# Decoding of weight pieces fenced behind the recurrence's copies, loads six and decodes three ahead

## The chip, the cores and the metric

The kernel runs on one core of a Trainium2 chip. The metric is the device time of one execution in microseconds; the median of three runs is compared.

## The reference

Two parts follow each other. The first is a recurrence over 768 steps for each of 4 batches and 8 heads, with a state of 40x40:

```
for t in range(S):
    y[:, :, t] = einsum('bhd,bhde->bhe', r_t, state)
    Sa = einsum('bhde,bhe->bhd', state, a_t)
    state = state * w_t[:, :, None, :] - einsum('bhd,bhe->bhde', Sa, b_t)
    state = state + einsum('bhd,bhe->bhde', v_t, k_t)
```

Its result, as 3072 tokens of 320 numbers, goes through two dense blocks with float64 weights: `h = ((x @ w1) * (x @ w2)) @ w3 @ w_out` (inner size 1024), and then `relu(h @ w_in) ** 2 @ w_out2` (inner size 2048).

## The kernel before, in words

The 768 steps are cut into 24 chunks of 32 steps, which are computed in closed form. A **preparation** of a chunk p reads its image (im, iw; L541, L551), scans the decay on VectorE (`prep_scan`: suf L556, gc L562, inv L564, wi L566), multiplies on GpSimd (`prep_mul`: L578, L584 four times), stores AW_d (L585, L586), and takes two products on TensorE (`prep_pq` L597 with the copies Pn on ScalarE L601, qt on VectorE L602 and GpSimd L604 and the store Q_d L605; `prep_kb` L614 with the copy kn on ScalarE L618 and the store KB_d L619). A **solve** (L645 to L668, VectorE) inverts the triangular matrices of four chunks at once (tmp L656, T L659, transposed into tt at L662); a **corner** (TensorE L690 and L693, ScalarE x L697 and tt L701) completes one chunk's inverse in the first four chunks.

The chain of a chunk c is: `do_x0` (TensorE L742, ScalarE copy X0 at L744), `do_sa` (L752, ScalarE copy SA at L754), `do_sat` (transposition L759, ScalarE copies vs L761 and YI L764 four times), `do_l` (L772, VectorE YI L777), `do_z` (L785, ScalarE YR L788; not in chunk 0), and `do_ys` (L800, VectorE RX L808, which is the state for the next chunk, and yst L812, stored to X_d at L815). `load_x`, `load_rv` and `load_y` fetch the next chunk's inputs.

Between the stages TensorE does other work, taken from a queue (`Fill`) by the nanoseconds of the tables GAP0 to GAPE: first the **fold** of w3 and w_out into one matrix (L462, sixteen pieces of w3 with four steps each), then the tiles of 256 tokens of the first dense block (`a_tile`: loads xf, xr L381 and L383; splits L357 to L360; products ab L370 with copies and products L401 and L402, gh and gl L407 and L408; px L428). TensorE's order is the program's order; on the other engines a scheduler places the instructions by priority and by its own times, and each engine then works in order. All loads and stores that appear below are issued in order by SP on one queue.

The weights come as 64-bit numbers and are **decoded** on the chip (`fetch`): a load by SP (L319), one ScalarE instruction for the high words (L325), one for the low words in place (L326), and two VectorE instructions that join them (L328, L330). A piece of w1, w2 or w_in is then split in two parts by ScalarE (L340, L353) and GpSimd (L341, L354). The tile that holds a raw piece is called raw or, where it borrows a place that is used later for something else, early; wst is the decoded piece. Before the change `fetch` does load and decoding in one call: five pieces of w3 ahead of the recurrence (W3_FIRST), one more per piece used, and the ten pieces of w1 and w2 in two batches, at the eighth and the thirteenth step of the fold (SPLIT_AT). The **change-over** to the second dense block (the loop that calls `split_w`, `split_r` and `wu` after the last chunk in the program) decodes w_in and w_out2; its first pieces find free buffers and are placed from chunk 3 on.

`FIRST` and `SECOND` are priorities of the stages and preparations; decoding has none:

```
            if kind == "decode":
                fn()
            else:
                with self.tc.high_priority(offset=FIRST):
                    fn()
```

`tc.issue_after(x)` keeps an instruction behind x in the order; before the change it is used for VectorE's decoding behind the first solve (`hold`).

## Time and profile before

| | |
|---|---|
| runs | 1069.87, 1073.65, 1074.45 us; median 1073.65 |
| profiled execution | 1071.28 us, span 1069.5 us, mean clock of TensorE 0.961 |
| busy | TensorE 918.1 us (86%), VectorE 712.5 (67%), ScalarE 443.8 (41%), GpSimd 233.2 (22%) |
| start of chunk (L742) | 0: 59.0; 1: 97.8; 2: 128.4; 3: 174.1; 4: 205.1; 5: 236.7; 12: 403.8; 13: 427.2; 23: 652.0 us |

A line of the timeline gives the start and the length of an instruction (or of a run of like ones) in microseconds, the engine, the line of the kernel, the operation, the tiles written and read, and in brackets how long the engine had been idle and what ended it. The engines are PE (TensorE), DVE (VectorE), ACT (ScalarE), POOL (GpSimd) and SP. An arrow with DMA means that a load or store ended the wait. The chunks are of unequal length in the beginning, 38.8 us for the first and 23 to 28 for those from the fifth on.

### The profile page before, as it was taken

How to read it: one execution, taken by the hardware profiler on the slowest of the kernel's cores; microseconds unless marked ns; L12 is line 12 of the kernel's file. 1: busy time of each engine (PE TensorE's matmuls, PEld its weight loads, DVE VectorE, ACT ScalarE, POOL GpSimd, SP SyncE). 2: the span in 40 equal slices, each digit the busy share in tenths (PEclk: the TensorE clock that was granted, in tenths of full speed). 3: DMA queues.
4: the chain of work that ended last, by engine and by line, in shares of the span. 5: the costliest groups of instructions: out<-in, count | busy, mean ns of one | idle time of the engine just before them, and what ended most of it. 6: DMA issues, size and time to landing. Idle time of an engine off the chain costs nothing.

```text
span 1069.5 us, 29225 instructions
## 1 busy us (share of the span) xinstructions
PE 918.1 (86%) x12240; PEld 822.5 (77%) x12240; DVE 712.5 (67%) x1399; ACT 443.8 (41%) x942; POOL 233.2 (22%) x304
## 2 busy tenths in 40 slices
PE   1327777688989889979899999889999999999997
PEld 1315545588888878979798889868989898898896
DVE  6864879957975997798489444887456554444432
ACT  2424556343434423424343434775334333333332
POOL 0271224433343343533200000652000000000000
PEclk9999888899999999989899999989999999999999
DMA  8976785666666567766644542665122121000001
GB/s 212 307 235 177 209 247 158 171 168 170 163 154 173 148 151 182 170 170 149 164 118 110 136 96 60 171 188 111 30 62 53 59 48 25 2 25 1 18 8 28
DMA packets 208922, 134.45 MB, mean 126 GB/s; under 512 B 143741, under 2 KB 184062, under 8 KB 208368
## 3 DMA queue, kind: packets, MB, share of 16 engines
q1 hardware_dynamic: 201424, 110.61, 40.6%
q0 software_dynamic: 7072, 21.57, 7.1%
q8 instruction: 99, 1.62, 0.7%
q10 hardware_dynamic: 288, 0.33, 0.2%
q14 instruction: 39, 0.32, 0.1%
HBM read 99.27 MB, written 33.19 MB: 124 GB/s over the span
## 4 chain that ended last, share of the span: by engine, by line
PE 48%; DVE 26%; DMA 12%; issue 5%; ACT 4%; POOL 3%; SPq 2%; ACTq 0%; DVEq 0%; POOLq 0%
PE ph L370 16%; PE po L997 15%; PE ab L370 6%; DMA im<-img 5%; DVE tmp L656 4%; PE px L428 4%; DVE T L659 4%; PE pat L800 2%; DVE RX L808 2%; DVE yst L812 2%; DVE gl L408 2%; DVE g L402 1%; DVE wst L328 1%; DVE YI L777 1%; POOL im L584 1%
## 5 line engine op out<-in xcount | busy, mean ns | idle before, releaser
L997 PE MATMUL po<-wul,rh 128*128 128x320 f32 x384 | 118.3, 308 | 0.0
L997 PE MATMUL po<-wuh,rh 128*128 128x320 f32 x384 | 118.0, 308 | 0.0
L997 PE MATMUL po<-wuh,rl 128*128 128x320 f32 x384 | 116.9, 308 | 0.0
L407 ACT CAST gh<-g 128x256 fp32r<-128x256 f32 x96 | 39.0, 406 | 99.8 <-DVE g L402 86.5
L370 PE MATMUL ph<-xh,wih 128*128 128x512 f32 x192 | 76.0, 396 | 0.7 <-issue 0.7
L428 PE MATMUL px<-wph,gh 128*128 128x320 f32 x192 | 68.1, 355 | 9.3 <-DVE x L433 4.8
L370 PE MATMUL ph<-xh,wil 128*128 128x512 f32 x192 | 75.7, 394 | 0.0
L370 PE MATMUL ph<-xl,wih 128*128 128x512 f32 x192 | 75.6, 394 | 0.0
L997 PEld LDWEIGHTS po<-wul,rh 128*128 128x128 f32 x384 | 72.0, 188 | 4.2
L997 PEld LDWEIGHTS po<-wuh,rh 128*128 128x128 f32 x384 | 72.0, 188 | 3.8
L997 PEld LDWEIGHTS po<-wuh,rl 128*128 128x128 f32 x384 | 71.6, 188 | 0.6 <-DVE rl L984 0.6
L800 PE MATMUL pat<-YI,YR 128*40 128x72 f32 (+1 forms) x1536 | 58.8, 240 | 13.7 <-DVE qt L602 8.1
L800 PEld LDWEIGHTS pat<-YI,YR 128*40 128x40 f32 x1536 | 54.5, 127 | 19.2 <-DVE qt L602 9.7
L408 DVE TENSOR_TENSOR gl<-g,gh 128x256 fp32r<-128x256 f32 x96 | 48.2, 503 | 30.0 <-ACT gh L407 29.6
L401 ACT COPY a_sb<-ab 128x256 f32<-128x256 f32 x96 | 35.6, 371 | 76.4 <-PE ab L370 75.9
L656 DVE TENSOR_TENSOR tmp<-PT,T 128x31 f32<-128x31 f32 (+20 forms) x170 | 64.9, 382 | 3.4
L659 DVE TENSOR_TENSOR T<-T,tmp 128x31 f32<-128x31 f32 (+20 forms) x170 | 64.5, 380 | 3.0
L428 PE MATMUL px<-wph,gl 128*128 128x320 f32 x192 | 63.2, 329 | 3.4 <-DVE gl L408 3.4
L584 POOL TENSOR_TENSOR im<-im,suf 104x256 f32<-104x256 f32 x80 | 64.4, 836 | 0.0
L428 PE MATMUL px<-wpl,gh 128*128 128x320 f32 x192 | 62.4, 325 | 0.0
L370 PE MATMUL ph<-xq,wir 128*128 128x512 f32 x192 | 60.1, 394 | 0.0
L370 PE MATMUL ab<-xh,w1h 128*128 128x256 f32 x192 | 57.9, 302 | 2.5 <-ACT xh L357 2.2
(539 smaller groups left out, 2444.3 us busy)
## 6 DMA issues: line engine op xcount, KB each, us to landing
...
```

What stands on the lines that cost most here:

```text
L370: mm(out=ps, lhsT=seq[i][0], rhs=seq[i][1], start=(i == 0), stop=(i == 7))
L401: act.copy(out=a_sb, in_=ps[:, 0])
L407: act.copy(out=t["gh"][:, ff], in_=g)
L408: dve.tensor_tensor(out=t["gl"][:, ff], in0=g, in1=t["gh"][:, ff], op=ALU.subtract)
L428: mm(out=ps, lhsT=a_, rhs=b_, start=(k == 0 and i == 0), stop=(k == 7 and i == 2))
L584: eng.tensor_tensor(out=kb[:, g, :, :, j], in0=kb[:, g, :, :, j], in1=sg, op=ALU.mult)
L656: dve.tensor_tensor(out=tv, in0=Pv[:, :, s, s + 1:n].unsqueeze(3).to_broadcast(sh), in1=Tv[:, :, s, 0:s + 1].unsqueeze(2).to_broadcast(sh) ...
L659: return dve.tensor_tensor(out=o, in0=o, in1=tv, op=ALU.subtract).ins
L800: mm(out=ps[64 * y:64 * y + D, b, 72 * z:72 * z + n], lhsT=YR[:, u], rhs=YI[:, u, 0:n], start=True, stop=True, tile_position=(0, 64 * y))
L808: dve.tensor_tensor(out=o, in0=v[r, :, :, C:72], in1=decay.unsqueeze(3).to_broadcast([D, 2, HZ, D]), op=ALU.mult)
L812: dve.tensor_tensor(out=yst[r, :, 2 * g:2 * g + 2].rearrange("p z b t -> p b z t"), in0=v[r, :, :, 0:C], in1=wt[c][r, 2 * g:2 * g + 2, :, ...
L997: mm(out=po[j][g], lhsT=a_, rhs=b_, start=(ff == 0 and i == 0), stop=(ff == 15 and i == 2))
```

## The change

It has five parts.

- In the table BETWEEN the products of preparation 5 (`("pq", 5)`) go from behind `do_x0` of chunk 0 to behind `do_ys` of chunk 0.
- `fetch` only loads; a new `decode` does the four instructions. w3 is loaded six pieces ahead and decoded three ahead (AHEAD). The ten pieces of w1 and w2 are loaded one per w3 piece from the fourth on (SPLIT_FROM), each decoded two pieces later.
- A fence: the copies X0, SA and YI put themselves into `fence`, and ScalarE's two instructions of a decode are issued after the last of these in program order (`behind(fence)`).
- The first a_tile's load and split count as decoding, and the split is fenced also; they stand in the queue ahead of the fold's last two columns ("last").
- For the change-over the fence is the last YI copy of chunk 12 (MID), so that ScalarE's decoding of w_in and w_out2 stands behind it.

```diff
@@ BETWEEN
-    (0, "x0"): (("corner", 0), ("pq", 5)),
+    (0, "x0"): (("corner", 0),),
@@
-    (0, "ys"): (("kb", 5), ("pq", 6), ("kb", 6)),
+    (0, "ys"): (("pq", 5), ("kb", 5), ("pq", 6), ("kb", 6)),
@@
-SPLIT_AT = (8, 13)
-W3_FIRST = 5
-FOLD_STAGED = 8
-SPLIT_STAGED = 8
+AHEAD = 3
+SPLIT_FROM = 3
@@ fetch, decode
-            hold = []
+            hold, fence = [], []
+            behind = lambda x: tc.issue_after(x[-1]) if x else nullcontext()
...
-                act.activation(out=o, in_=hi.bitcast(F32), func=AF.Copy, scale=2.0 ** -112)
-                act.activation(out=lo, in_=lo, func=AF.Copy, scale=2.0 ** -29, bias=LOW)
-                with tc.issue_after(hold[-1]) if hold else nullcontext():
+                with behind(fence):
+                    act.activation(out=o, in_=hi.bitcast(F32), func=AF.Copy, scale=2.0 ** -112)
+                    act.activation(out=lo, in_=lo, func=AF.Copy, scale=2.0 ** -29, bias=LOW)
+                with behind(hold):
                     dve.scalar_tensor_tensor(out=ou, in0=ou, scalar=3, in1=lo, op0=ALU.logical_shift_left,
                                              op1=ALU.bitwise_or)
@@ a_tile
                 def split():
+                  with behind(fence if n == 0 else ()):
...
-                fill.push((0, load, "load"), (0, split, "load"), before="x")
+                fill.push((0, load, "load" if n else "decode"), (0, split, "load" if n else "decode"),
+                          before="x" if n else "last")
@@ fold
+                for i in range(3):
+                    load_w3(i)
...
+                for i in range(AHEAD):
+                    decode_w3(i)
+                    load_w3(i + 3)
...
+                for i in range(16):
+                    f = i // 2
+                    for k in range(4 * (i % 2), 4 * (i % 2) + 4):
+                        items.append((FOLD_NS, lambda f=f, k=k: step(f, k), "last" if f > 5 else "w"))
+                    if i + AHEAD < 16:
+                        then(decode_w3, i + AHEAD)
+                    if i + AHEAD + 3 < 16:
+                        then(load_w3, i + AHEAD + 3)
+                    m = i - SPLIT_FROM
+                    if 0 <= m - 2 < 10:
+                        then(decode12, m - 2)
+                    if 0 <= m < 10:
+                        then(load12, m)
@@ do_x0, do_sa, do_sat
-                    act.activation(out=X0, in_=ps[:, 0, 0:320].rearrange("p (h d) -> p h d", d=D),
-                                   func=AF.Copy, scale=-1.0)
+                    fence[:] = [act.activation(out=X0, in_=ps[:, 0, 0:320].rearrange("p (h d) -> p h d", d=D),
+                                               func=AF.Copy, scale=-1.0).ins]
...
+                        fence[:] = [act.copy(out=YI[96:128, H * b:H * b + H, C:72],
+                                             in_=SA[32 * b:32 * b + 32, :, 0:D]).ins]
+                    if c == MID:
+                        mid.extend(fence)
@@ change-over
+            fence[:] = mid
...
-                for k in range(2):
-                    split_w(wst, win, wih, wil, j, k)
+                todo = [piece_w(win, wih, wil, 256, j, k) for k in range(2)]
...
+                for load, split in todo:
+                    split(decode(wst, load(wst)))
```

What this does to the order of the engines shows at three places.

ScalarE, chunk 0, from the copies of preparation 4 to SA; before (L326 are low words of w_out and w3, early and raw their tiles):

```order
L601 COPY Pn<-pat 128x2x4x32
L326 ACTIVATE early<-early 128x512
L618 COPY kn<-pat 128x8x40 x2
L326 ACTIVATE early<-early 128x512
L744 ACTIVATE X_101<-pat 128x320
L697 ACTIVATE x_683<-pat 128x128
L701 COPY tt<-pat 16x8x16 x4
L325 ACTIVATE wst<-raw 128x512
L326 ACTIVATE raw<-raw 128x512 x3
L601 COPY Pn<-pat 128x2x4x32
L326 ACTIVATE raw<-raw 128x512
L754 COPY SA<-pat 128x8x40
```

And with the change, where the numbers of the lines are some 16 higher (L760 is X0, L770 SA, L781 YI, L778 vs):

```order
L617 COPY Pn<-pat 128x2x4x32
L634 COPY kn<-pat 128x8x40 x2
L760 ACTIVATE X_101<-pat 128x320
L713 ACTIVATE x_675<-pat 128x128
L717 COPY tt<-pat 16x8x16 x4
L770 COPY SA<-pat 128x8x40
L781 COPY YI<-SA 32x8x40 x4
L778 COPY vs<-pat 104x4x4x32
```

The five decoding instructions between Pn and SA and the second Pn copy, that of preparation 5, are gone from here.

VectorE, chunk 0, around the copy YI (L777 before, L797 with the change; L566 and L582 are wi, L808 and L828 are RX). Before:

```order
L566 SCALAR_TENSOR_TENSOR wi<-iw,inv 104x528
L602 STREAM_TRANSPOSE qt<-pat 128x256
L556 SCALAR_TENSOR_TENSOR suf<-iw,mark 104x529
L562 SCALAR_TENSOR_TENSOR gc<-suf 104x16
L564 RECIPROCAL inv<-gc 104x16
L566 SCALAR_TENSOR_TENSOR wi<-iw,inv 104x528
L777 TENSOR_TENSOR YI<-pat,msk 64x8x2x32 x2
L808 TENSOR_TENSOR RX<-pat,gc 40x8x40 x2
```

With the change:

```order
L582 SCALAR_TENSOR_TENSOR wi<-iw,inv 104x528
L797 TENSOR_TENSOR YI<-pat,msk 64x8x2x32 x2
L572 SCALAR_TENSOR_TENSOR suf<-iw,mark 104x529
L578 SCALAR_TENSOR_TENSOR gc<-suf 104x16
L580 RECIPROCAL inv<-gc 104x16
L582 SCALAR_TENSOR_TENSOR wi<-iw,inv 104x528
L828 TENSOR_TENSOR RX<-pat,gc 40x8x40 x2
```

YI stands ahead of the preparation's second scan now, but still behind the first wi; RX is still behind both.

ScalarE, chunk 12, from SA on (L764 and L781 are YI, L761 and L778 vs, L407 and L404 gh of the activation tile). Before:

```order
L754 COPY SA<-pat 128x8x40
L764 COPY YI<-SA 32x8x40
L401 COPY a_sb<-ab 128x256
L764 COPY YI<-SA 32x8x40 x3
L761 COPY vs<-pat 104x4x4x32
L407 CAST gh<-g 128x256
L401 COPY a_sb<-ab 128x256
L407 CAST gh<-g 128x256
```

With the change (L315 high and L316 low words of w_in and w_out2):

```order
L781 COPY YI<-SA 32x8x40 x3
L315 ACTIVATE wst<-raw 128x256
L316 ACTIVATE raw<-raw 128x256
L315 ACTIVATE wst<-raw 128x256
L316 ACTIVATE raw<-raw 128x256
L315 ACTIVATE wst<-raw 128x256
L316 ACTIVATE raw<-raw 128x256
L315 ACTIVATE wst<-raw 128x320
L316 ACTIVATE raw<-raw 128x320 x2
L778 COPY vs<-pat 104x4x4x32
L404 CAST gh<-g 128x256
L398 COPY a_sb<-ab 128x256
```

Nine decoding instructions, which stood in chunks 3 and 4, are now between YI and vs of chunk 12.

## Rows read from the trace of the kernel before

**Rows 1.** Busy time by stretch, chunks 0, 2, 3, 12 (from:to, length, engines)
```profile
59.00:97.80 38.80, 18.58 (x632) 16.07 (x632) 21.67 (x38) 10.83 (x27) 15.39 (x10) 1.00 0.66 174
...
128.40:174.10 45.70, 34.00 (x511) 24.29 (x512) 39.30 (x76) 25.22 (x49) 17.27 (x17) 0.81 0.75 223
...
174.10:205.10 31.00, 22.92 (x380) 17.65 (x381) 30.29 (x59) 13.60 (x29) 11.17 (x12) 0.94 0.56 146
...
403.80:427.20 23.40, 21.48 (x409) 20.13 (x411) 15.63 (x30) 9.75 (x23) 9.23 (x15) 0.93 0.71 179
```

**Rows 2.** Timeline of TensorE, chunks 0 to 4 (start, length, ..., idle before)
```profile
72.59 1.18 PE L597 MATMUL pat<-im 40*32 40x64 f32 x64 [9.93 <-POOL im L578]
...
83.25 1.10 PE L759 MATMUL pat<-idt,SA 128*104 128x128 f32 x4 [8.26 <-ACT SA L754]
...
143.10 1.09 PE L759 MATMUL pat<-idt,SA 128*104 128x128 f32 x4 [6.05 <-ACT SA L754]
...
221.85 1.15 PE L772 MATMUL pat<-RT,vs 104*64 104x64 f32 x32 [1.72 <-ACT vs L761]
```

**Rows 3.** Timeline of VectorE, chunks 0 to 4
```profile
80.12 1.26 DVE L566 TENSOR_TENSOR_SCAN wi<-iw,inv 104x528 f32<-104x528 f32 x1 [2.80 <-DMA AW_d<-wi]
...
83.99 1.26 DVE L556 TENSOR_TENSOR_SCAN suf<-iw,mark 104x529 f32<-104x529 f32 x1 [2.27 <-DMA iw<-img]
...
87.78 1.39 DVE L777 TENSOR_TENSOR YI<-pat,msk 64x512 f32<-64x512 f32 x2 [0.67 <-PE pat L772]
...
91.45 0.99 DVE L808 TENSOR_TENSOR RX<-pat,gc 40x320 f32<-40x320 f32 x2 [2.29 <-PE pat L800]
...
137.09 0.69 DVE L328 SCALAR_TENSOR_TENSOR wst<-wst,raw 128x512 uint32<-128x512 uint32 x1 [2.10 <-DMA im<-img]
...
153.32 1.39 DVE L777 TENSOR_TENSOR YI<-pat,msk 64x512 f32<-64x512 f32 x2
...
213.77 0.60 DVE L662 STREAM_TRANSPOSE tt<-T 128x256 f32<-128x256 f32 x1
```

**Rows 4.** The chain of waits, 55 to 240 us (start, length, what)
```profile
71.95 8.07 DMA AW_d<-wi
...
98.95 7.54 DMA im<-img
...
216.90 3.92 DMA raw<-win
```

**Rows 5.** Timeline of ScalarE, chunks 1 to 4
```profile
101.54 0.76 ACT L618 COPY kn<-pat 128x320 f32<-128x320 f32 x2 [4.29 <-DMA KB_d<-kn]
...
197.41 0.43 ACT L325 ACTIVATE wst<-raw 128x256 f32<-128x256 f32 x1 [2.79 <-DMA raw<-win]
...
197.75 0.43 ACT L326 ACTIVATE raw<-raw 128x256 uint32<-128x256 uint32 x1
...
205.65 0.49 ACT L325 ACTIVATE wst<-raw 128x320 f32<-128x320 f32 x1 [5.15 <-DMA raw<-wo]
...
220.90 0.43 ACT L326 ACTIVATE raw<-raw 128x256 uint32<-128x256 uint32 x1 [1.75 <-DMA raw<-win]
```

**Rows 6.** Timeline of ScalarE, chunk 12
```profile
411.91 0.59 ACT L761 COPY vs<-pat 104x512 f32<-104x512 f32 x1
```

**Rows 7.** Timeline of VectorE, chunk 12
```profile
415.06 0.68 DVE L777 TENSOR_TENSOR YI<-pat,msk 64x512 f32<-64x512 f32 x1 [0.74 <-PE pat L772]
```

**Rows 8.** Timeline of TensorE, chunk 12
```profile
413.86 1.15 PE L772 MATMUL pat<-RT,vs 104*64 104x64 f32 x32
```

**Rows 9.** Timeline of GpSimd, preparations 5, 6 and 8
```profile
55.45 6.79 POOL L584 TENSOR_TENSOR im<-im,suf 104x256 f32<-104x256 f32 x4
...
62.21 5.58 POOL L604 TENSOR_TENSOR qt<-qt,msk 128x256 f32<-128x256 f32 x1
...
82.59 0.72 POOL L604 TENSOR_TENSOR qt<-qt,msk 128x256 f32<-128x256 f32 x1
...
139.61 3.25 POOL L584 TENSOR_TENSOR im<-im,suf 104x256 f32<-104x256 f32 x4
```

126 lines of the change are left out of this document (59 added, 67 removed).

## The prediction

> **What bounds the kernel now.** I read the busy time by stretch first, one stretch per chunk of the recurrence, and then the timelines of the engines inside the stretches that the change touches. Chunk 0 takes 38.8 us and no engine is busy for more than 22 of them [rows 1]: that stretch is bound by waits. Chunk 2 takes 45.7 us with VectorE busy for 39.3, chunk 3 takes 31.0 with VectorE busy for 30.3 [rows 1]: there VectorE bounds. Chunk 12 takes 23.4 us with TensorE busy for 21.5 [rows 1]: from chunk 5 on TensorE bounds, and every microsecond that it is made to wait is added to the end.
>
> The waits of chunk 0 are two rows of TensorE: it stands 9.93 us before the products of preparation 5 (L597), for which GpSimd has no operand ready, and 8.26 us before the transposition of SA (L759), because ScalarE is late with the SA copy [rows 2]. ScalarE is late since it stands in four low-word instructions, each waiting for its w3 load. Chunk 2 has the same wait once more, 6.05 us [rows 2]. These 24.2 us are what the change goes for. The reader should also see VectorE in chunk 0: wi(6) at 80.12 waits 2.80 us for a store, suf(7) at 83.99 waits 2.27 us for a load, YI(0) starts at 87.78 and RX(0) at 91.45 [rows 3]. And in chunk 12 vs, L772 and YI follow each other closely on three engines, with no wait of TensorE before L772 [rows 6 to 8].
>
> The sum is made against the profiled execution, 1071.28 us; the median of the runs, 1073.65, lies 2.4 us above it. The forecast shifts the median. I take 0.5% (5.4 us) as what a measurement of this kernel can tell from no change.
>
> **The change, part by part.**
>
> Chunk 0. The products of preparation 5 go behind chunk 0, and the decoding goes off ScalarE there, so both TensorE waits go: 18.2 us. But YI(0) on VectorE now has wi(6) ahead of it, and RX(0) has suf(7), gc, inv and wi(7), as the order shows. wi(6) starts when the store AW_d<-wi has landed, 8.07 us after its issue at 71.95 [rows 4]; three w3 loads still stand ahead of that store on SP's queue, so I leave it at 80.12. Then YI(0) runs at 81.4 instead of 87.78, suf(7) still waits for its load until 83.99, and wi(7) ends 3.1 us later (1.26, 0.6 for gc and inv, 1.26), at 87.1. RX(0) starts there instead of at 91.45. **Of 18.2 us, 4.35 are kept**; what is late next is the store. Bounds: 0 and 18.2; I take 4.35, since its three waits are rows.
>
> Start of chunk 1. Four preparation steps now run back to back behind chunk 0. There is one buffer qt, so its second copy waits for the store of the first, which on SP's queue stands behind two weight loads and a KB_d store; before, the kn copy waited 4.29 us for a KB_d store and held X0(1) until 102.18 [rows 5]. I expect X0(1) at about the same time. The image load for preparation 7, issued at 98.95 and 7.54 us long [rows 4], goes out some 4 us sooner, but six decoding instructions of 0.69 us [rows 3], 4.1 us, now stand between its suf and YI(1), where two stood before (1.4 us), and gc, inv and wi with them. **Gain of chunks 0 and 1: 0**, bounds -1 and 4.35.
>
> Chunk 2. The 6.05 us wait goes. YI(2) at 153.32 is however not set by SA: VectorE has waited only 6.4 us since the solve began, in waits such as the 2.10 before 137.09 [rows 3], and the change leaves it as much work there (43 entries of the order where 40 stood, decoding for w1 and w2 among them). suf(9) hangs on its image load, about 4 us sooner, so that some of these idle times shrink. **I take 0.5 us**, bounds 0 and 3.
>
> Chunks 3 and 4. VectorE's work from YI(2) to YI(3) is two decoding instructions more and three of the solve fewer: no change. From YI(3) to the transposition tt at 213.77 [rows 3], on which chunk 4 hangs, eight change-over instructions go (3.6 us by their 0.43 to 0.49), four decoding ones of 0.69 come (2.7 us), and the solve has some 1.2 us more to do; but VectorE no longer stands behind the 5.15 us that ScalarE waited for the load of wo2 [rows 5], of which I take 1.3 off: 1 us sooner. Then the 1.72 us before L772(4) go, where ScalarE stood in the change-over's low-word instruction waiting 1.75 us for its load [rows 2, 5]. **Gain 2.7**, bounds 0 and 5. By chunk 5 the sum is **-3.2 us** (bounds +1 and -9).
>
> Chunk 12. The change-over's first four pieces are decoded here. On ScalarE nine instructions stand between the YI copies and vs(12): six of 0.43 and three of 0.49 us, each starting 0.34 us after the one before where nothing is waited for [rows 5]. That is 3.2 us, at most 4.1. vs(12) moves from 411.91 to 415.1 and L772 from 413.86 [rows 6, 8] to 415.7: +1.85. Behind vs stands one more low-word instruction, whose load is issued in this chunk behind those of the activation tile; ahead of it nothing may pass, so the gh cast behind it is late, and on VectorE gl stands ahead of YI(12). With a load of 3.92 us [rows 4], issued at about 414, ScalarE goes on at 418, gl ends at 418.9, and YI(12) starts there instead of at 415.06 [rows 7]. TensorE has no slack: **+3.7 us**, bounds 1.9 (no wait for the load) and 7 (a wait like the 5.15 us one [rows 5]). The changed positions on GpSimd and the five loads more on SP in chunk 12 are covered: GpSimd is busy for 9.23 of the 23.4 us [rows 1], and SP's loads are not waited for before the one counted.
>
> The sum is -3.2 + 3.7 = +0.5 us, about 1072 for a profiled execution, **1074 for the median: no change that can be measured.** By the bounds of the terms that are not excluded the case reaches from 1069 to 1079.
>
> **Rivals.**
>
> *A, faster: the early gain carries through.* If the store and image loads land some 4 us sooner because no weight decode holds the loads of w3 back, chunk 1 keeps its 4.35 us, the solve starts as much sooner, and YI(2) follows, since VectorE is then merely shifted. With 2.7 us of chunks 3 and 4 and 1.9 lost in chunk 12: 1.5 for a shorter chain in chunk 2 added, -4.4 - 1.5 - 2.7 + 1.9 = -6.7, **1067**; with the full bounds 1063. For it: VectorE is idle for 17 of 38.8 us in chunk 0 [rows 1], so there is room. Against it: VectorE's order has fewer entries ahead of YI(2) than before, so work was put off, not drawn ahead.
>
> *B, slower: ScalarE's wait for a load in chunk 12.* The five loads are issued late, and ScalarE's order lets nothing past. If the first of them lands 5 us after ScalarE is free (as at 205.65 [rows 5]) and the later ones cost TensorE as much again through gh and gl, chunk 12 loses 8 to 10 us: **1080**. It decides from a loss of 8.6 us on (3.2 gained, 5.4 more). For it: in chunks 3 and 4 the same instructions waited 2.79, 5.15 and 1.75 us for their loads [rows 5]. Against it: all that TensorE then lost to a late vs was 1.72 us [rows 2].
>
> *C, slower: VectorE's decoding against GpSimd's preparation.* Four products of GpSimd took 6.79 us at 55.45 and 3.25 at 139.61; the mask product 5.58 at 62.21 and 0.72 at 82.59 [rows 9]; the long ones ran beside unbroken decoding on VectorE. The change gathers decoding in chunks 1 to 3, where YI waits for suf and suf for GpSimd. One preparation stretched by 8.4 us (3.54 and 4.86) there gives **1082**, and it decides if decoding runs unbroken while GpSimd is on the chain. Against it: 3.25 us with decoding all around. The Trainium skill ("SBUF — State Buffer", Who interferes with whom) says that a VectorE instruction with two SBUF inputs contends with a GpSimd instruction that reads SBUF, one blocking the other whole. The rows above agree, and by that rule each decoding instruction that meets GpSimd costs one of the two its length: with the six of chunk 1 at 0.69 us the sum would be +4.6 instead of +0.5.
>
> *D: it doesn't do what it says.* The fence only ties decoding to the previous copy, and decoding still stands right ahead of SA in chunk 2, so its wait may stay; then the sum is +1 to +4, **1077**.
>
> **How the numbers follow.** My forecast 0.42 and D 0.08 lie within 0.5%: same 0.50. A 0.28: faster, since most of my terms are set by single waits and gains may add up. B 0.15 and C 0.07: slower 0.22. The range takes A to 1064 and B and C to 1082, leaving out about 2 in 10 at the ends; the likeliest case alone has 1069 to 1079.
>
> **What would show it.** Right: L742(1) still starts at 97 to 100 us, L759(0) has no long wait, YI(2) starts at 152 to 153, L772(4) at 218 to 220 without ScalarE ahead of it, and chunk 12 is 27 us long in place of 23.4, with waits for vs and YI. Wrong: YI(2) before 150 (A), chunk 12 above 30 us (B), a row of four products of GpSimd above 5 us in chunks 1 to 3 (C), or a wait for SA above 4 us in chunk 2 (D). A changed busy time of TensorE in the later stages would mean that I have missed something that the order does not show.

## The result, and the profile after

The change makes the kernel slower: median 1084.2 us (1083.7 to 1087.55, four runs) against 1074.05 (four runs), a ratio of 1.0103 [1.0078, 1.0127], or some 10 us. The profiled execution took 1083.7 us (span 1081.9, mean clock of TensorE 0.956), where the one before took 1071.28. The forecast was 1074, no change that can be measured, with a range from 1064 to 1082: the result lies outside it. The ratio of e18 below leaves out one of its twelve executions, which took 1464.64 us at a mean granted clock of 0.581.

The starts of the chunks say where the time went. Line numbers are those of the changed kernel here: L758 begins a chunk, L797 is YI, L792 the matmul before it, L778 vs, L315 and L316 ScalarE's decoding, L634 kn, L618 qt.

| chunk | 0 | 1 | 2 | 3 | 4 | 5 | 12 | 13 | end |
|---|---|---|---|---|---|---|---|---|---|
| before, us | 59.0 | 97.8 | 128.4 | 174.1 | 205.1 | 236.7 | 403.8 | 427.2 | 1069.5 |
| after, us | 59.1 | 102.8 | 130.7 | 179.6 | 213.0 | 244.2 | 409.5 | 439.8 | 1081.9 |
| after minus before | +0.1 | +5.0 | +2.3 | +5.5 | +7.9 | +7.5 | +5.7 | +12.6 | +12.4 |

Some 7.5 us are lost by the start of chunk 5, chunks 5 to 11 give 1.8 back, and 6.9 more are lost in chunk 12; from chunk 13 to the end both kernels take 642 us. The same stretches as in [rows 1] (from:to, length, then TensorE matmuls, weight loads, VectorE, ScalarE, GpSimd, each with its count, then granted clock, DMA share, GB/s), for chunks 0 to 4 and 12:

```profile
59.10:102.80 43.70, 18.87 (x632) 15.78 (x632) 19.90 (x33) 8.04 (x23) 14.96 (x12) 0.91 0.71 194
102.80:130.70 27.90, 23.34 (x476) 17.26 (x476) 14.79 (x27) 11.67 (x25) 4.47 (x6) 0.83 0.58 163
130.70:179.60 48.90, 35.67 (x511) 25.69 (x510) 39.79 (x78) 30.29 (x60) 17.66 (x13) 0.76 0.72 206
179.60:213.00 33.40, 24.74 (x384) 18.65 (x384) 32.83 (x55) 16.53 (x32) 17.43 (x18) 0.90 0.53 136
213.00:244.20 31.20, 25.91 (x420) 24.20 (x420) 18.60 (x43) 10.98 (x26) 10.04 (x16) 0.84 0.66 169
...
409.50:439.80 30.30, 23.50 (x409) 21.42 (x411) 18.78 (x39) 14.18 (x36) 9.71 (x17) 0.89 0.72 183
```

Chunk 0 is 4.9 us longer although VectorE and ScalarE have less to do in it; chunk 12 is 30.3 us long where it was 23.4. The waits of TensorE that the change went for [rows 2] are gone, and others stand in their place; in chunk 0 it is 7.04 us before L820 at 82.22, right behind YI(0). TensorE's timeline after, with the idle time and its end in brackets:

```profile
102.80 1.29 PE L758 MATMUL pat<-RX,XL 128*32 128x40 f32 x64 [9.21 <-ACT kn L634]
...
137.34 0.60 PE L776 MATMUL pat<-idt,SA 128*104 128x128 f32 x4
147.84 1.98 PE L792 MATMUL pat<-RT,vs 104*64 104x64 f32 x32 [6.55 <-ACT vs L778]
...
172.19 4.07 PE L820 MATMUL pat<-YI,YR 128*40 128x72 f32 x64 [5.06 <-DVE qt L618]
...
222.54 1.29 PE L768 MATMUL pat<-X,tt 32*32 32x40 f32 x64 [4.59 <-DVE inv L580]
229.35 1.15 PE L792 MATMUL pat<-RT,vs 104*64 104x64 f32 x32
...
421.05 1.15 PE L792 MATMUL pat<-RT,vs 104*64 104x64 f32 x32 [2.91 <-ACT vs L778]
```

The transposition of SA at 137.34 has no wait where 6.05 us stood; ten microseconds later vs costs 6.55. The row at 229.35 has lost the 1.72 us of before, and the one ahead of it waits 4.59 us where it waited 1.58. (The row names inv; the transposition tt, on which it hangs, ends just before it.) The same matmul before:

```profile
214.52 1.29 PE L752 MATMUL pat<-X,tt 32*32 32x40 f32 x64 [1.58 <-DVE tt L662]
```

VectorE after, to be laid beside [rows 3, 7]:

```profile
79.44 1.26 DVE L582 TENSOR_TENSOR_SCAN wi<-iw,inv 104x528 f32<-104x528 f32 x1 [10.53 <-DMA AW_d<-wi]
80.73 1.39 DVE L797 TENSOR_TENSOR YI<-pat,msk 64x512 f32<-64x512 f32 x2
...
86.48 0.99 DVE L828 TENSOR_TENSOR RX<-pat,gc 40x320 f32<-40x320 f32 x2
...
102.36 0.45 DVE L618 STREAM_TRANSPOSE qt<-pat 128x256 f32<-128x256 f32 x1 [11.65 <-DMA Q_d<-qt]
...
125.98 0.99 DVE L828 TENSOR_TENSOR RX<-pat,gc 40x320 f32<-40x320 f32 x2 [5.73 <-PE pat L820]
...
142.96 1.26 DVE L572 TENSOR_TENSOR_SCAN suf<-iw,mark 104x529 f32<-104x529 f32 x1 [5.48 <-POOL im L600]
...
155.09 1.39 DVE L797 TENSOR_TENSOR YI<-pat,msk 64x512 f32<-64x512 f32 x2
...
166.19 0.69 DVE L318 SCALAR_TENSOR_TENSOR wst<-wst,early 128x512 uint32<-128x512 uint32 x1 [2.45 <-ACT wst L315]
...
196.81 1.39 DVE L797 TENSOR_TENSOR YI<-pat,msk 64x512 f32<-64x512 f32 x2
...
221.79 0.60 DVE L678 STREAM_TRANSPOSE tt<-T 128x256 f32<-128x256 f32 x1
...
426.54 1.39 DVE L797 TENSOR_TENSOR YI<-pat,msk 64x512 f32<-64x512 f32 x2
```

YI(0) comes 7 us earlier than before (80.73 against 87.78), YI(1) at 115.96 (114.52 before), YI(2) at 155.09 (153.32), YI(3) at 196.81 (191.22), tt at 221.79 (213.77). The two rows of before that [rows 3] lack:

```profile
114.52 1.39 DVE L777 TENSOR_TENSOR YI<-pat,msk 64x512 f32<-64x512 f32 x2
...
191.22 1.39 DVE L777 TENSOR_TENSOR YI<-pat,msk 64x512 f32<-64x512 f32 x2
```

The gain of chunk 0 ends two rows further down: VectorE stands 11.65 us before the second qt copy, since the store of the first is late. ScalarE has the same for kn:

```profile
102.00 0.75 ACT L634 COPY kn<-pat 128x320 f32<-128x320 f32 x2 [8.86 <-DMA KB_d<-kn]
...
420.43 0.57 ACT L778 COPY vs<-pat 104x512 f32<-104x512 f32 x1
...
425.35 0.44 ACT L316 ACTIVATE raw<-raw 128x256 uint32<-128x256 uint32 x1 [3.77 <-DMA raw<-win]
```

What the two stores stood behind is read from SP's own queue (start of the issue and how long it takes; two loads of 512 KB each, then the stores):

```profile
93.05 0.84 SPq L301 DMA_DIRECT2D early<-w  x2
93.99 0.37 SPq L635 DMA_DIRECT2D KB_d<-kn  x1
94.46 0.38 SPq L621 DMA_DIRECT2D Q_d<-qt  x1
...
419.77 2.30 SPq L301 DMA_DIRECT2D raw<-win  x4
```

The copies that wait for the stores start at 102.00 and 102.36, eight microseconds after the issue. The Trainium skill ("DMA: Bandwidth & Descriptors", Queues, rings and completion order) says that each DMA engine takes the descriptors of a ring in their order, and that the signal of a transfer's end lands only behind the earlier writes of that engine. This case agrees: the KB_d store takes 7.91 us from its issue to its end here, and 3.65 us in e2 below, where no weight load is issued right ahead of it. The last row is the load for which ScalarE waits at 425.35; it takes 5.47 us from its issue.

Where VectorE's time went, between three of its rows, from the sums of the timeline's rows (neighbouring rows overlap by tenths, so the sums can pass the length):

| stretch | length before, after | decoding | other work | idle |
|---|---|---|---|---|
| YI(1) to YI(2) | 38.80, 39.13 | 10.8, 8.9 | 22.5, 19.7 | 7.7, 12.7 |
| YI(2) to YI(3) | 37.90, 41.72 | 19.6, 19.1 | 20.3, 22.3 | 0.5, 3.1 |
| YI(3) to tt of chunk 4 | 22.55, 24.98 | 3.8, 2.7 | 18.7, 23.7 | 1.3, 0.0 |

In the first stretch VectorE idles 5 us more than before, in the two rows of 5.73 and 5.48 us above, and does 4.7 us less work; that work then stands in the next two stretches, where VectorE has no slack. Over the three stretches VectorE idles 6.3 us more than before and works 0.7 more; with the 1.4 us by which YI(1) is late, the idle time makes 7.7 of the 8.0 us by which tt is late.

### The profile page after: what moved, and what is told of

Read it like the earlier page. It is cut to its first block, busy times and chain, and to the rows that moved or that the text cites. A ratio compares the mean times of both kernels' runs of the same rounds, so it can differ in the third digit from the quotient of the medians.

```text
span 1081.9 us, 29216 instructions
## 1 busy us (share of the span) xinstructions
PE 920.9 (85%) x12240; PEld 823.0 (76%) x12240; DVE 711.0 (66%) x1399; ACT 441.9 (41%) x942; POOL 235.0 (22%) x304
## 3 DMA queue, kind: packets, MB, share of 16 engines
q8 instruction: 98, 1.61, 0.7%
## 4 chain that ended last, share of the span: by engine, by line
PE 47%; DVE 26%; DMA 11%; ACT 5%; issue 4%; SPq 3%; POOL 3%; ACTq 0%; DVEq 0%; POOLq 0%
PE ph L366 16%; PE po L1023 15%; PE ab L366 6%; DVE T L675 4%; DVE tmp L672 4%; PE px L425 3%; DVE RX L828 2%; DVE yst L832 2%; DMA im<-img 2%; PE pat L820 2%; POOL im L600 2%; DVE wst L320 2%; DVE gl L405 2%; DVE g L399 2%; DMA AW_d<-wi 1%
## 5 line engine op out<-in xcount | busy, mean ns | idle before, releaser
L404 ACT CAST gh<-g 128x256 fp32r<-128x256 f32 x96 | 38.9, 405 | 106.6 <-DVE g L399 93.7
L820 PE MATMUL pat<-YI,YR 128*40 128x72 f32 (+1 forms) x1536 | 58.8, 240 | 23.1 <-DVE qt L618 14.5
L820 PEld LDWEIGHTS pat<-YI,YR 128*40 128x40 f32 x1536 | 54.3, 127 | 28.7 <-DVE qt L618 16.4
L675 DVE TENSOR_TENSOR T<-T,tmp 128x31 f32<-128x31 f32 (+20 forms) x170 | 68.7, 404 | 3.1
L405 DVE TENSOR_TENSOR gl<-g,gh 128x256 fp32r<-128x256 f32 x96 | 44.9, 468 | 29.5 <-ACT gh L404 29.1
L399 DVE TENSOR_TENSOR g<-a_sb,ab 128x256 f32<-128x256 f32 x96 | 39.8, 415 | 31.2 <-ACT a_sb L398 30.2
```

The lines of the kernel that those rows point to most:

```text
L399: dve.tensor_tensor(out=g, in0=a_sb, in1=ps[:, 1], op=ALU.mult)
L404: act.copy(out=t["gh"][:, ff], in_=g)
L405: dve.tensor_tensor(out=t["gl"][:, ff], in0=g, in1=t["gh"][:, ff], op=ALU.subtract)
L675: return dve.tensor_tensor(out=o, in0=o, in1=tv, op=ALU.subtract).ins
L820: mm(out=ps[64 * y:64 * y + D, b, 72 * z:72 * z + n], lhsT=YR[:, u], rhs=YI[:, u, 0:n], start=True, stop=True, tile_position=(0, 64 * y))
```

## The experiments

Each ratio is against runs of the kernel before on the same chip in the same session. "The change" as a base means the changed kernel.

### Where the loss lies

**e1_mid_off**: the change, with the change-over's decoding not fenced.

```diff
-            fence[:] = mid
+            fence[:] = []
```

> The changed kernel without the fence behind chunk 12: the change-over's decoding may go where buffers allow, in chunks 3 to 5 again. Theory (three waits: a KB_d store behind two weight loads at the start of chunk 1, VectorE in chunks 2 and 3, a load wait in chunk 12): chunk 12 is 23 to 24 us long in place of 30.2, chunks 3 and 4 get 1.5 to 3 us longer, median 1078 to 1081. Rival (the loss of chunk 12 is only where a loss of the decoding shows, it comes back wherever the decoding goes): chunks 3 to 5 get 6 us longer, 1083 to 1085.

Ratio 1.0195 [1.0159, 1.0230]: slower still. Chunk 12 has its old length again, but chunk 4 takes 38.3 us instead of 31.2 (windows of chunks 4 and 12):

```profile
214.80:253.10 38.30, 26.69 (x420) 24.94 (x420) 22.39 (x51) 15.65 (x39) 10.22 (x17) 0.82 0.65 169
418.90:442.10 23.20, 20.50 (x409) 18.63 (x408) 14.49 (x31) 9.67 (x23) 9.30 (x16) 1.00 0.70 164
```

TensorE in chunk 4 of this run:

```profile
236.75 1.51 PE L792 MATMUL pat<-RT,vs 104*64 104x64 f32 x32 [4.45 <-ACT vs L778]
```

In this profile the loss of 7 us moved from chunk 12 to chunk 4. The profiled execution is the fastest of six (1085.91 us; their median is 1092.34), so what makes the median so much slower is not seen in it, and both forecasts were too low.

**e2_kbd_first**: the change, with the loads of w1 and w2 issued behind the KB_d store of preparation 6. **e3_both** is e1 and e2 together; **e5_w3_late** is e3 with the second three loads of w3 behind that store as well.

```diff
-                    q_["prep"].dma_start(out=KB_d[c], in_=kn.rearrange("p g z y e -> p (g z y e)"))
+                    st = q_["prep"].dma_start(out=KB_d[c], in_=kn.rearrange("p g z y e -> p (g z y e)")); late.extend([st.ins] if c == 6 else [])
...
-                    loaded[m] = w12s[m][0](wf, staged(ma, ("gh", "gl"), 1024))
+                    with behind(late): loaded[m] = w12s[m][0](wf, staged(ma, ("gh", "gl"), 1024))
```

and in e5, on top of it and of e1's edit:

```diff
-                    w3[i] = fetch(wf, 4, 128, [(slice(0, 128), slice(0, 4), wcols(w3t, 128 * f, 128)[
+                    with behind(late): w3[i] = fetch(wf, 4, 128, [(slice(0, 128), slice(0, 4), wcols(w3t, 128 * f, 128)[
...
-                    load_w3(i + 3)
...
+                for i in range(3, 6): then(load_w3, i)
```

> The changed kernel with the loads of w1 and w2 issued behind the KB_d store of preparation 6. Theory: the second kn copy behind chunk 0 waits 2 to 4 us in place of 8.9, L758 of chunk 1 starts at 97 to 99 us in place of 102.8, and this is still there at chunk 5: median 1079 to 1081. Rival (VectorE's decoding alone sets chunks 2 to 4, the start of chunk 1 does not count): L758 of chunk 1 at 97 to 99, but of chunk 4 at 212 to 213 as before: 1084.

> Both edits together, no fence behind chunk 12 and the loads of w1 and w2 behind KB_d of preparation 6. Theory: the two add up, 1073 to 1076, level with the kernel before. Rival (VectorE alone sets the early chunks): as without the fence of chunk 12 alone, 1078 to 1081.

> As both edits together, and the second three w3 loads also behind the KB_d store of preparation 6, so that the store AW_d of preparation 5 has no weight load ahead of it. Theory (chunk 0 hangs on that store): it lands about 3 us after its issue instead of 6.6, wi(6) starts near 75 us, L758 of chunk 1 near 93, and the median is 3 to 5 us below both edits: 1069 to 1072. Rival (VectorE alone): wi(6) and L758 sooner, but chunk 4 where both edits have it, within 1 us of them. Third case: the fold stands without its pieces in chunk 1, since they are loaded 25 us later, and it is slower than both edits by 3 or more.

Ratios 1.0116 [1.0066, 1.0165], 1.0089 [1.0041, 1.0136], 1.0072 [1.0034, 1.0110]. In e2 the cause of the late copy is confirmed, and most of the gain does not follow at the start of chunk 1 (ScalarE, then VectorE):

```profile
100.20 0.75 ACT L634 COPY kn<-pat 128x320 f32<-128x320 f32 x2 [3.76 <-DMA KB_d<-kn]
```

```profile
86.47 1.39 DVE L797 TENSOR_TENSOR YI<-pat,msk 64x512 f32<-64x512 f32 x2
```

The wait falls from 8.86 to 3.76 us, but with other positions on SP's queue VectorE's order changed too: YI(0) went behind the next scan, to 86.47. Chunk 1 starts at 101.0, 100.7 and 100.3 us in the three runs (102.8 with the change, 97.8 before). In e1 and e9, which differ from the change only in the change-over and have the same order of VectorE in chunk 0, it starts at 105.2 and 105.7, so a difference of 2 us is within what single profiles scatter; what the wait for the store is worth shows in e10. The forecast of e5, that wi(6) would start near 75 us with no weight load ahead of its store, missed: it starts at 80.74. The three intervals overlap with the change's: no verdict between them. Between e1 and e3, which differ by e2's edit, there is one, since 1.0195 [1.0159, 1.0230] and 1.0089 [1.0041, 1.0136] lie apart: chunk 4 takes 30.6 us in e3 where it took 38.3. So with the change-over's pieces in chunk 4 the later loads of w1 and w2 are worth about 1%; by which wait was not followed up.

**e6_split0**: w1 and w2 from the first piece of the fold on, to draw decoding ahead of YI(2).

```diff
-SPLIT_FROM = 3
+SPLIT_FROM = 0
```

> The changed kernel with the pieces of w1 and w2 loaded from the first w3 piece on (SPLIT_FROM 0 in place of 3), so that VectorE's order has 47 decoding instructions ahead of YI(2), as the kernel before, in place of 41. Theory V (the change has put VectorE's decoding off from chunks 0 and 1, where it idles, to chunks 2 to 4, which it bounds): x0(4) starts near 209 us in place of 213.0, median 1079 to 1081. Rival (single waits for loads and stores set the early chunks, wherever the decoding stands): x0(4) within 1.5 us of 213, median 1083 to 1086.

Ratio 1.0112 [1.0044, 1.0180]. Six more decoding instructions stand ahead of YI(2), chunk 3 shrinks to 31.0 us, and chunk 2 grows to 51.9:

```profile
133.90:185.80 51.90, 33.48 (x509) 23.08 (x509) 42.98 (x84) 28.57 (x58) 18.93 (x18) 0.83 0.64 184
185.80:216.80 31.00, 23.53 (x382) 18.08 (x383) 29.74 (x58) 14.47 (x29) 13.09 (x14) 0.89 0.55 137
```

Decoding that is drawn ahead is paid for in chunk 2; chunk 4 starts at 216.8, later than with the change. My forecast missed.

**e7_no_fence**: the change without the recurrence's fence (`gate` is empty until the change-over).

```diff
-                with behind(fence):
+                with behind(fence if gate else ()):
...
-            fence[:] = mid
+            fence[:] = mid; gate.append(1)
```

> The changed kernel with ScalarE's decoding free of the fence during the recurrence (the fence behind chunk 12 stays). VectorE's order has 36 and 47 decoding instructions ahead of YI(1) and YI(2), in place of 28 and 41. Theory V: chunk 2 lasts 44 to 46 us in place of 48.9, x0(4) at 206 to 209, median 1078 to 1081, even if TensorE waits for SA again. Rival (the fence keeps off waits that cost more): waits for SA above 5 us come back and the median is 1085 or more.

Ratio 1.0161 [1.0100, 1.0221]. Chunks 2 and 3 have their old lengths (45.6 and 31.4 us) and chunk 1 takes 33.9 instead of 27.9; chunk 4 starts at 215.9. The forecast of theory V (chunk 4 at 206 to 209 us, 1078 to 1081) missed: with as much decoding ahead of YI(2) as in the kernel before, chunks 2 and 3 win back what they lost, and chunks 0 and 1 lose more. Within the whole change the fence does not cost; if anything it helps, though this interval and the change's overlap.

### The parts, one at a time

**e8_pq_only**: the kernel before with one entry of the table moved.

```diff
-    (0, "x0"): (("corner", 0), ("pq", 5)),
+    (0, "x0"): (("corner", 0),),
...
-    (0, "ys"): (("kb", 5), ("pq", 6), ("kb", 6)),
+    (0, "ys"): (("pq", 5), ("kb", 5), ("pq", 6), ("kb", 6)),
```

> The kernel before with the products of preparation 5 moved behind chunk 0, and nothing else. Theory V: VectorE's decoding stands as before, so that this part is worth nothing or a little, 1070 to 1075. Rival K (with the move the second kn copy stands behind the KB_d store, which waits in the queue behind weight loads): x0(1) at 101 us or later, in place of 97.8, and 1077 or more.

Ratio 1.0120 [1.0046, 1.0194]: this move alone costs about as much as the whole change, within a wide interval. TensorE, and ScalarE, at the start of chunk 1 (L742 begins the chunk and L618 is kn, since the line numbers are those of the kernel before):

```profile
104.87 1.29 PE L742 MATMUL pat<-RX,XL 128*32 128x40 f32 x64 [10.11 <-ACT kn L618]
```

```profile
100.65 0.66 ACT L325 ACTIVATE wst<-early 128x512 f32<-128x512 f32 x1 [6.34 <-DMA early<-w]
...
104.08 0.74 ACT L618 COPY kn<-pat 128x320 f32<-128x320 f32 x2
```

The same two loads stand ahead of the same store on SP's queue, but the store is not what holds kn last: without the fence the copy stands in ScalarE's order behind the decoding of the two pieces, for whose load ScalarE waits 6.34 us, and it runs right behind that decoding. In the same way vs waits behind a low word that waits 2.55 us for its load at 120.23, and YI(1) starts at 124.25 (114.52 before). Chunk 1 starts 7.1 us later than before, and chunk 5, at 244.2, 7.5 later.

**e4_pq_back**: the change with that entry back in its old place (the diff above, reversed).

> The changed kernel with the products of preparation 5 back behind do_x0 of chunk 0; fence, loads and change-over as changed. Theory K (what the early chunks lose comes from this move: four preparation steps in a row behind chunk 0, with one buffer each for qt and kn, wait for stores that stand behind weight loads): x0(1) starts at 95 to 98 us in place of 102.8, chunk 5 at 236 to 240 in place of 244.2, median 1076 to 1080, with the loss of chunk 12 left. Rival V (decoding put off on VectorE, 41 instructions ahead of YI(2) here too): chunk 5 within 2 us of 244, 1083 to 1086.

Ratio 1.0081 [1.0045, 1.0117]. Chunk 1 starts at 97.6, chunk 3 at 174.4, as before; then chunk 3 takes 34.8 us instead of 31.0 and chunk 5 starts at 239.3 (+2.6). With chunk 12 (29.4 us, +6.0) that makes 8.6 us. The ratio's 0.81% are 8.7 us, but this agreement is luck: chunks 4 to 11 give some back, chunk 13 starts 7.8 us later than before, and the profiled execution (1085.14 us; the median is 1081.38) loses 6.0 us more from there to the end. Up to chunk 13, what is left without the move is in chunks 3 and 12.

**e10_two_bufs**: the change, with a second place for qt and kn in preparation 6, so that no copy waits for a store.

```diff
-qt = first(c, "qt", [128, 2, HZ, C], {1: (at, "yst"), 3: (at, "yst")})
+qt = first(c, "qt", [128, 2, HZ, C], {1: (at, "yst"), 3: (at, "yst"), 6: (wa, "w2r")})
...
-kn = first(c, "kn", [128, 2, HZ, 2, D], {1: (at, "rt"), 3: (at, "vs")})
+kn = first(c, "kn", [128, 2, HZ, 2, D], {1: (at, "rt"), 3: (at, "vs"), 6: (wa, "w1r")})
```

> The changed kernel with a second buffer for qt and for kn, used by preparation 6, so that its copies wait for no store. Theory K: x0(1) starts at 94 to 97 us, with no wait of ScalarE or VectorE for a KB_d or Q_d store ahead of it, chunk 5 at 237 to 242, median 1077 to 1081. Rival V: x0(1) as early, but chunk 5 within 2 us of 244, 1083 to 1086.

Ratio 1.0166 [1.0106, 1.0226]: slower, not faster. Chunk 1 starts at 95.5 us, 7.3 earlier than with the change, and YI(1) comes at 116.14, where it was (115.96). GpSimd and VectorE say why it did not move:

```profile
105.24 1.19 POOL L594 TENSOR_TENSOR im<-im,wi 104x512 f32<-104x512 f32 x1 [9.51 <-DMA im<-img]
```

```profile
109.05 1.26 DVE L572 TENSOR_TENSOR_SCAN suf<-iw,mark 104x529 f32<-104x529 f32 x1 [14.12 <-POOL im L600]
```

GpSimd waits for the image of preparation 7, and VectorE for GpSimd. In this profile YI(1) does not hang on the start of chunk 1, but on this load, which is issued at 96.13 behind two weight loads. Why the kernel is slower than the change is not seen in the recurrence: chunk 13 starts at 436.8 us, 3.0 sooner than with the change, and the time is lost behind it (below).

**e17_prep_behind_l**: the kernel before with the fence, and the scans of preparations 6 and 7 placed behind YI(0).

```diff
-    (0, "start"): (("prep", 5), ("prep", 6)),
+    (0, "start"): (("prep", 5),),
...
-    (0, "l"): (("corner", 1, 1),),
+    (0, "l"): (("corner", 1, 1), ("prep", 6)),
...
-                    dve.tensor_tensor_scan(
+                    with behind(y0[1:2] if c in (6, 7) else ()): dve.tensor_tensor_scan(
```

> The kernel before with ScalarE's fence of the recurrence, preparation 6 behind do_l of chunk 0, and its first scan behind YI(0), so that YI(0) waits for no store. Theory (chunk 0 hangs on YI(0) behind the scan, chunk 1 on the image load of preparation 7, chunk 3 on VectorE): YI(0) starts at 78 to 82 us in place of 87.8 and x0(1) at 91 to 95, but YI(1) within 2 us of 114.5, and the median is within 3 us of the fence alone. Rival (chunk 0's time is carried through): YI(1) 3 us or more sooner, and the median 4 us or more below the fence alone.

Ratio 1.0048 [1.0022, 1.0074]. YI(0) comes at 83.8 us instead of the 87.5 of the fence alone (e14, next), but chunk 1 starts at 97.5 (97.1 there), not at 91 to 95, and YI(1) at 114.1: of an earlier YI(0) nothing is carried into chunk 1. The kn copy behind chunk 0 waits for its store as before (4.24 us, 4.63 in e14).

**e14_fence_only**: the kernel before with the fence behind X0, SA and YI; it is lifted for the change-over.

```diff
-                act.activation(out=o, in_=hi.bitcast(F32), func=AF.Copy, scale=2.0 ** -112)
-                act.activation(out=lo, in_=lo, func=AF.Copy, scale=2.0 ** -29, bias=LOW)
+                with behind(fence): act.activation(out=o, in_=hi.bitcast(F32), func=AF.Copy, scale=2.0 ** -112)
+                with behind(fence): act.activation(out=lo, in_=lo, func=AF.Copy, scale=2.0 ** -29, bias=LOW)
...
-                    act.copy(out=SA[:, :, 0:D], in_=ps[:, 0, 0:320].rearrange("p (h d) -> p h d", d=D))
+                    fence[:] = [act.copy(out=SA[:, :, 0:D], in_=ps[:, 0, 0:320].rearrange("p (h d) -> p h d", d=D)).ins]
...
-            early = False
+            early = False; fence.clear()
```

> The kernel before with ScalarE's decoding fenced behind the last X0, SA or YI copy, and nothing else (no move of preparation 5, loads and change-over as before). VectorE's order then has 28 and 41 decoding instructions ahead of YI(1) and YI(2), in place of 31 and 47. Theory V (the fence puts VectorE's decoding off into chunk 3): the wait for SA in chunk 2 is under 2 us in place of 6.05, but chunk 3 lasts 33 to 35 us in place of 31.0, median 1073 to 1078. Rival (the fence is the good part, the others spoil it): chunk 3 at 31 to 32 us, median 1066 to 1071.

Ratio 1.0015 [0.9979, 1.0052]: no difference. This is the cleanest picture of the change's intention. Chunks 1 to 3:

```profile
97.10:125.80 28.70, 21.88 (x480) 15.88 (x482) 14.69 (x26) 13.19 (x29) 4.94 (x6) 0.88 0.81 229
125.80:167.60 41.80, 33.20 (x511) 23.67 (x512) 34.70 (x70) 26.35 (x52) 14.56 (x14) 0.84 0.75 222
167.60:206.00 38.40, 27.81 (x380) 21.85 (x380) 37.13 (x67) 18.04 (x35) 18.22 (x18) 0.78 0.54 126
```

Against [rows 1], chunk 2 falls from 45.7 to 41.8 us with VectorE's busy time falling from 39.30 to 34.70, and chunk 3 starts 6.5 us earlier than before. Chunk 3 then takes 38.4 instead of 31.0 with VectorE busy for 37.13, where it was 30.29. All of the gain is given back in one chunk, by the engine that bounds it. What moved out of chunk 2 is mostly the solve: its L656 and L659 take 13.5 us in chunk 2 before and 10.0 in e14, and 10.5 and 15.6 us in chunk 3. TensorE in chunks 2 and 3:

```profile
141.03 1.15 PE L772 MATMUL pat<-RT,vs 104*64 104x64 f32 x32 [3.18 <-ACT vs L761]
...
181.80 1.98 PE L772 MATMUL pat<-RT,vs 104*64 104x64 f32 x32 [4.09 <-ACT vs L761]
```

In chunk 2 the 6.05 us for SA became 3.18 us for vs, a copy that is not itself in the fence, and chunk 3 has 4.09 us for vs.

**e15_mid_only** and **e15b_mid_only**: the kernel before with the change-over's decoding behind the YI copies of chunk 12. In e15 the YI copies of the four batches are left out in chunks 13 to 23; e15b, whose edit is shown (with the decode's two instructions behind the fence as in e14), has them.

```diff
-                        act.copy(out=YI[96:128, H * b:H * b + H, C:72], in_=SA[32 * b:32 * b + 32, :, 0:D])
+                        yc = act.copy(out=YI[96:128, H * b:H * b + H, C:72], in_=SA[32 * b:32 * b + 32, :, 0:D]); mid.extend([yc.ins] if c == 12 else [])
...
-            early = False
+            early = False; fence[:] = mid
```

> The kernel before with the change-over's decoding fenced behind the last YI copy of chunk 12, and nothing else. Theory: chunk 12 lasts 27 to 30 us in place of 23.4, by a wait of ScalarE for a load issued in that chunk and by nine instructions ahead of vs; chunks 3 and 4 together are 0 to 3 us shorter than 62.6; median 1074 to 1079. Rival (what chunk 12 loses was gained in chunk 4): the median is 1070 to 1073.

> The change-over's fence alone once more, on the kernel before and now with the YI copies of chunks 13 to 23, which the kernel e15_mid_only left out. Theory: chunk 12 loses what it lost there (29.3 us in place of 23.4) and chunk 4 wins what it won there (27.1 in place of 31.6), so that this part is worth nothing: 1072 to 1077. Rival (that kernel's time was short by the copies left out): 1078 or more.

Ratios 0.9989 [0.9959, 1.0020] and 0.9977 [0.9956, 0.9999]. The second is the fastest kernel of the study, though by less than the 0.5% that I called measurable. Chunks 4 and 12 of e15b, and ScalarE in chunk 12:

```profile
205.40:232.70 27.30, 25.04 (x424) 23.39 (x427) 17.88 (x36) 10.98 (x26) 10.20 (x17) 0.87 0.69 176
398.10:425.90 27.80, 22.88 (x405) 21.21 (x404) 18.41 (x39) 14.20 (x36) 9.28 (x16) 0.88 0.73 181
```

```profile
413.38 0.44 ACT L326 ACTIVATE raw<-raw 128x256 uint32<-128x256 uint32 x1 [3.10 <-DMA raw<-win]
```

Chunk 4 takes 27.3 us instead of 31.6, chunk 12 27.8 instead of 23.4: 4.3 saved, 4.4 spent.

**e9_mid_two**: the change, with the fifth piece of the change-over and all behind it fenced behind YI of chunk 14, so that its load is not waited for in chunk 12.

```diff
-                    if c == MID:
+                    if c in (MID, MID + 2):
...
-            fence[:] = mid
+            fence[:] = mid[0:1]; n_u = 0
...
-                    split(decode(wst, load(wst)))
+                    n_u += 1; fence[:] = mid[0:1] if n_u <= 4 else mid[1:2]; split(decode(wst, load(wst)))
```

> The changed kernel with the first four pieces of the change-over behind YI of chunk 12, as there, and all later ones behind YI of chunk 14. Theory (chunk 12 loses by low-word instructions that wait for loads issued in the same chunk): the 3.77 us wait goes, chunk 12 lasts 25 to 27 us in place of 30.3, chunk 14 at most 1 longer, median 1079 to 1081. Rival (the nine instructions ahead of vs, and VectorE's eight, make the loss): chunk 12 still lasts 29 to 31 us.

Ratio 1.0110 [1.0072, 1.0147]. Chunk 12:

```profile
410.10:434.30 24.20, 20.02 (x405) 18.60 (x404) 17.90 (x39) 12.21 (x31) 9.26 (x16) 1.00 0.83 218
```

It takes 24.2 us instead of 30.3, and the wait for the load is gone. The clock differs too, 1.00 here and 0.89 with the change; in e4 and e11 (below), which differ by the same edit, chunk 12 takes 29.4 us at 0.88 and 27.2 at 0.87. So the load is worth from 2.2 to 6.1 us, and how much of the rest is the nine instructions and how much the clock was not separated. The profiled span fell by 3.7 us, the median by 2.4 and the ratio not at all.

**e11_pq_back_mid_two** is e4 with e9's edit, **e12_pq_back_mid_off** e4 with e1's (the diffs of those). **e18_fence_mid_two** is e14 with the change-over's pieces behind YI of chunks 12 and 14:

```diff
+                if not early: nu[0] += 1; fence[:] = mid[3:4] if nu[0] <= 4 else mid[7:8]
```

> The products of preparation 5 back behind do_x0 of chunk 0, and the change-over's later pieces behind chunk 14. Theory (early loss by the move, late loss by load waits in chunk 12, and these two are all): chunk 5 at 236 to 240, chunk 12 lasts 24 to 25 us, median 1070 to 1075, at least level with the kernel before. Rival V: 1078 to 1082.

> The products of preparation 5 back behind do_x0 of chunk 0, and no fence for the change-over. Theory: chunks 4 and 5 together are 4 to 7 us longer than in the kernel before (54.9), by the change-over's decoding, chunk 12 23 to 24 us, median 1074 to 1080. Rival (that loss in chunk 4 came from the late early chunks alone): chunks 4 and 5 together at 55, median 1069 to 1073.

> The kernel before with ScalarE's fence of the recurrence and the change-over's first four pieces behind YI of chunk 12, all later ones behind YI of chunk 14; no move of preparation 5, loads and decodes as before. Theory (VectorE bounds chunks 2 to 4, and what leaves it there is won): chunk 4 lasts 26 to 28 us in place of 31.6, chunk 12 24 to 27 us, median 1067 to 1071, below the kernel before. Rival (the decoding costs the same wherever it goes): 1072 to 1076.

Ratios 1.0068 [1.0037, 1.0100], 1.0152 [1.0106, 1.0198] and 1.0045 [1.0025, 1.0066]. In e12 chunk 4 takes 41.3 us, more still than in e1. All nine low words of the change-over's first pieces stand in chunk 4 in both, where before there were six. But they do so in e14 also, which takes 31.6 us there at a granted clock of 0.95 (0.82 in e1, 0.71 in e12), so their number alone does not explain it. In e18 chunk 3 takes 38.4 us, as in e14, and chunks 12 and 14 28.4 and 31.2; chunk 5 starts at 231.9, 4.8 us sooner than before, and all of that is gone by chunk 13 (427.3). None beats the kernel before.

**e16_ahead_only**: the change without the move and without either fence, so that the loads six ahead, the decoding three ahead and the single pieces of w1 and w2 are left (with the other places in the queue that belong to them).

```diff
-                with behind(fence):
+                with behind(fence if gate else ()):
...
-            fence[:] = mid
+            fence[:] = []
```

> The changed kernel with the products of preparation 5 back in chunk 0 and without both fences: what is left is loads six and decodes three ahead, and w1 and w2 piece by piece. VectorE's order has 31 and 47 decoding instructions ahead of YI(1) and YI(2), as the kernel before. Theory V: chunk 3 lasts 31 to 32 us; the waits for SA are back; median 1071 to 1077. Rival (the new places of the loads cost by themselves): chunks 0 to 3 are 4 us or more longer than before, 1078 or more.

Ratio 1.0063 [1.0036, 1.0090]. Up to chunk 4 (206.8 us) it stays within 1.7 us of the kernel before; then chunk 4 takes 37.4 us (31.6 before):

```profile
216.03 1.29 PE L768 MATMUL pat<-X,tt 32*32 32x40 f32 x64 [4.86 <-DVE tt L678]
226.92 1.98 PE L792 MATMUL pat<-RT,vs 104*64 104x64 f32 x32 [3.87 <-ACT vs L778]
```

That is the loss which e1 and e12 show too; the fence behind chunk 12 takes it from chunk 4 and puts it into chunk 12.

Alone, then, the parts give +1.20% (move), +0.15% (fence), +0.63% (ahead) and -0.23% (change-over behind chunk 12). Their sum is +1.75%, against +1.03% for the whole; with the intervals as wide as they are the two are not apart. Putting the move back takes off only 0.2%, with overlapping intervals. That the parts compete for the same VectorE time in chunks 2 to 4 is an argument, which no run tests; a model in which they add up is not to be had from these runs.

One thing blurs all these ratios. The stretch from chunk 13 to the end, with the same number of matmuls, some 6200, lasts 642.4 us before and 642.1 after, but from 640.5 (e15b) to 653.5 us (e7) in the profiles of the experiments. In e2, e7, e10, e11, e17 and e18 TensorE waits 3.8 to 4.8 us there, at the start of the second dense block, for GpSimd's split of w_out2, where its wait is 0.7 us before and after; what else differs is open. So a ratio does not tell what an edit did in the recurrence; the rows of its stretch do. e2, for one, starts chunk 5 at 238.3 us and chunk 13 at 430.1, 5.9 and 9.7 us sooner than the change, and loses 7.0 of that behind chunk 13.

## Why the prediction was wrong

- **Chunk 0: right.** YI(0) was forecast at 81.4 us and RX(0) at 87.1; measured 80.73 and 86.48. Both of its waits in [rows 2] went. (Of ScalarE's four low words only three waited for a load, 1.90, 1.12 and 1.61 us; the longest wait there, 10.87 us at 74.66, is that of the high word ahead of them.) That it came so close is in part luck: with the same order of VectorE, YI(0) starts at 83.87 in e1 and 83.93 in e9.
- **Start of chunk 1: the term was mis-sized.** "I expect X0(1) at about the same time" named the two loads and the store that the kn copy would stand behind; the price taken was the old 4.29 us [rows 5], and it was 8.86. X0(1) started at 104.16, 2 us later than the 102.18 before. The gain of chunks 0 and 1 was put at 0 with a bound of -1; the start of chunk 2 lost 2.3. e10, where chunk 1 starts 7.3 us sooner and YI(1) does not, shows that an earlier start alone gains nothing at YI(1).
- **Chunk 2: the SA wait went, and D with it.** YI(2) was to come 0.5 us sooner and came 1.8 later; 1.4 of them YI(1) had already. TensorE's 6.55 us for vs were not foreseen.
- **Chunks 3 and 4: the step that failed.** The prediction put the work that VectorE puts off at nothing: "the change leaves it as much work there (43 entries of the order where 40 stood, decoding for w1 and w2 among them)" counted entries of VectorE's order as if they would run when they stood there. VectorE idled 12.7 us between YI(1) and YI(2) instead of 7.7, and 4.7 us less work got done ahead of YI(2). "No change" from YI(2) to YI(3) was +3.8: 2.0 of other work and 2.6 of idling, most of it 2.45 us for a high word that ScalarE had not yet decoded. From YI(3) to tt I counted 1.2 us more of the solve; other work there grew by 5.0, and the "1 us sooner" was 2.4 later. By the start of chunk 5 I forecast -3.2 and +7.5 was measured: 10.7 of the error of 12 us. e14 shows the deferral by itself, on the kernel before: VectorE's busy time falls by 4.7 us in chunk 1 and 4.6 in chunk 2, and rises by 6.8 in chunk 3, mostly the solve. There it only takes back what the fence had gained; that it is also what makes the whole change lose is read from the profile. e7, which undoes it in the changed kernel, loses the time in chunks 0 and 1 instead, and e4 lays 4.9 of the 7.5 us at chunk 5 to the move of preparation 5.
- **Chunk 12: right mechanism, too small a size.** Forecast +3.7 with an upper bound of 7, measured +6.9. vs and L792 wait as described, and the load for the fifth piece is issued when I took it to be: at 419.77, where the 414 of the forecast becomes 419.8, since the chunk starts 5.8 us later. The term that was too small is the load's time, 5.47 us where 3.92 was taken. YI(12) starts 17.0 us behind the start of its chunk instead of 11.3, +5.7, and from there to chunk 13 another 1.2 us are lost.
- **Rivals.** A fell: YI(2) did not come before 150. C fell: the rows of four GpSimd products in chunks 1 to 3 are 2.61, 2.63 and 3.52 us long. B's mechanism is there, and its sign, chunk 12 above 30 us, came with 30.3; it costs 6.9 us where it needed 8.6 to decide, and alone (e15b) it is balanced by chunk 4. D's wait for SA is gone. In the profile the loss comes from VectorE's deferred work and from chunk 12 together. No rival had the first as a loss: the argument against A names it ("work was put off, not drawn ahead") and gives it no price.
- **The bounds.** The gains of the terms up to chunk 5 add up to bounds of -12.35 and +1, not -9 and +1; with those of chunk 12 the case reaches from 1063 to 1082 and not only from 1069 to 1079. The result lies above either.

What stays open: why VectorE idles in the changed kernel where it did not before, beyond the rows that end its waits; what the ratios owe to the stretch behind chunk 13; whether the parts add up; whether any order of VectorE in chunks 2 to 4 would keep chunk 2's 3.9 us of e14 (none that was run did); and how much of the ratios of 0.2 to 0.4% is the clock, below.
